# One order of a fused attention and token-mixer kernel replaced by another, its first loads kept

## The chip, the cores and the metric

The kernel runs on one core of a Trainium2 chip. The metric is the device time of one execution in microseconds, the median of several runs. The names of the engines here: PE multiplies matrices (PEld is its loading of weights), DVE and ACT work on elements, POOL is a slower engine for elements, SP issues most of the DMAs. PE writes to PSUM, of which the kernel uses eight banks; everything else lies in SBUF.

## The reference, cut to what matters

```
mod = silu(c) @ w_mod               # six rows of 512: sa, ca, ga, sb, cb, gb
h = layernorm(x) * (1 + ca) + sa    # x: 2048 tokens x 512
x = x + ga * A(h)
h = layernorm(x) * (1 + cb) + sb
x = x + gb * B(h)
# A: q, k, v = h @ wqkv, 32 heads of 16; token s attends to s, s-2, ..., s-14
#    logits = q.k / 4, masked where the index is negative; softmax over 8; times v; @ wo
# B: h = layernorm(h); u = gelu(h^T @ w1 + b1)   # over the 2048 tokens, to 1792
#    y = u @ w2 + b2, transposed back            # 1792 to 2048 tokens
```

All matrices are bf16. B mixes tokens: its first product needs every token of h before any column is complete.

## The kernel before, in words

**Tiles and stages.** The 2048 tokens are 16 tiles of 128 (st 0 to 15), in five chunks of 2, 4, 4, 4 and 2 tiles (SIZES, line 267). For each chunk `build_chunk` (lines 616 to 913) lists: the statistics of a layernorm (ln1s, ln1v, rstd1, nb1) and the normalised tile (n1); its transpose, by PE for chunks 0 and 1 (tr, hT) and by DMA for the others (xt); q, k and v (qkv, with t = 0, 1, 2) and their evacuation from PSUM (ev); the products of q with the eight shifted keys on DVE (qk, four to a chunk) and their sum over a head's 16 elements by PE (red, into the two banks psL); the maximum (max, DVE), its subtraction by PE (sub), the exponential on ACT (exp), its sum (esum), the reciprocal by logarithm and exponential (rcp, ACT), the scaling (smB, DVE), and DMAs that lay the weights out anew (a2). The values are shifted by DMA (vd). DVE multiplies weights by values (pv, four to a chunk), PE sums (pvacc), ACT copies the result to o_sb (oev), and PE multiplies by wo and adds x (wo). Then come the second layernorm (x1, ln2q, ln2m, rstd2, nb2, n2), its scaling (aff) and the third (ln3s, ln3v, rstd3, nb3, h3). The qk and pv of the four-tile chunks work on 128 x 4096 elements, those of chunks 0 and 4 on 128 x 2048.

**The token mixer** is interleaved (lines 925 to 1040): mlp1_L_F_S multiplies by w1 for block F of 14, in sweeps L over the tokens (0 to 5, 6 to 10, 11 to 15 for blocks 0 to 6; 0 to 9, 10 to 15 for the others), from tile S on; a finished sweep is parked in SBUF (park), added (padd) and put through gelu. mlp2_T multiplies by w2 for output tile T, fin adds the bias and x, st_out stores. The sweeps that start at tile 10 or 11 need h3_10 to h3_15.

**Start.** The condition c is loaded (ld_c), turned by PE (cps), and made silu(c) by an exponential on ACT (silu_exp) and three small operations on DVE (silu_dve, tile sc). modcols1 multiplies it by the 512 columns of w_mod for 1 + ca; a1col is that column, by which hT and the copies of wqkv (wsc) are scaled. modrow, mrows, st_row, ld_row and woq_s bring the other rows of mod to all partitions.

**What sets the order.** Every operation is put into a graph with the tiles that it reads and writes; `schedule` (lines 86 to 125) then emits the operations in the order of a handwritten list, ORDER (lines 191 to 249), and each engine executes its own in that order. A token is a name and a tag: `:a`, `:d`, `:p`, `:s` choose ACT, DVE, POOL or SP where an operation has alternatives. On PE `q` splits a 128-column weight load and matmul into four of 32 columns side by side (`mm`, line 522), as red, pvacc, modrow and mask always are; `n` takes the alternative without one of its matmuls. `fill:n` emits idle matmuls of n pieces of 128 columns, four pieces to one matmul (line 528); they write to a free bank and nobody reads them. Ring buffers (six PSUM banks, four `big`, five `vd`) are given out in the order of the list too, so a token's place also sets what it waits for. `locks` marks operations of DVE and is not used by `schedule`.

ld_c is added at line 429, on ACT's queue. `dma2` (line 381) adds a DMA that can go on SP's or ACT's queue.

Of the kernel before, what the change touches and what calls it, by code (L numbers as in the profile page):

```python
# [206 lines left out]
oev0_2:a qkv2_11 qkv2_02:q ev2_03:a qk2_3 qkv2_01:q red2_0 oev0_0:a wo0:q wsc2_1:a wsc2_2:a qkv2_12 ev2_11:a ev2_01:a
ev2_02:a ev2_12:a wo1 qkv2_21:q a2_1_1:a qkv2_22 x1_1:a ln2q1:a x1_0:a xt10 ln2q0:a qk2_1 qkv2_23 xt12 qk2_2 a2_1_0:s
halo_k3:a ln2m0 vd1_2 a2_1_2:s qkv3_12 a2_1_3:s pv1_2 rstd1_4 red2_1 nb1_4 vd1_0 st_row1 red2_2 red2_3 rstd2_0
ev2_22:a nb2_0 ev2_21:a qkv3_13:q ev3_13:a max2 vd1_3 pv1_0 n1_14:a vd1_1 pvacc1_2 n1_15:a qkv2_20:q ev2_20:a sub2  # L210
qkv3_22:q ev3_12:a pv1_1 qkv3_10 exp2 ev2_23:a halo_v3:a qkv3_20 n2_0:a oev1_2:a ev3_10:a esum2 rcp2 qkv3_00 ev3_22:a
# [10 lines left out]
oev3_1:a mlp1_0_2_0:q pv3_0 mlp1_0_2_2:q nb3_4 h3_4:a mlp1_0_0_0:q mlp1_0_0_2 h3_5:a mlp1_0_0_4:q qk4_0 ln2q8:a
ln2q6:a park0_0:a ln2q9:a mlp1_0_6_4:q mlp1_0_2_4:q mlp1_0_1_4:q park0_1:a pv3_2 mlp1_0_5_4:q vd3_3 pvacc3_0 oev3_0:a
mlp1_0_3_4:q ld_w2_1 park0_2:a pv3_3 red4_0 ln2m6 pvacc3_2 oev3_2:a mlp1_0_4_0:q qk4_1 pvacc3_3 ld_w1_0_1152
mlp1_0_4_2:q mlp1_0_4_4:q rstd2_6 oev3_3:a wo12:q halo_v4:p vd4_2 vd4_3 nb2_6 n2_9:a qk4_2 n2_7:d qk4_3 wo10:qn red4_1
ld_w1_0_1408 n2_6:a vd4_1 n2_8:a aff6 red4_2 red4_3 max4 park0_3:a ln3s8:d ln3s6:d x1_12:a ln3v8 wo11 vd4_0 ln3s9:d
mlp1_0_7_0 ld_w2_3 park0_4:a ln3v6 mlp1_0_7_2 park0_5:a ln3v9 x1_11:a ln2q12:a mlp1_0_8_0 mlp1_0_8_2 park0_6:a wo13:n
ln3s7:a ln3v7 sub4 mlp1_0_10_0 mlp1_0_9_0 x1_13:d exp4 rstd3_6 nb3_6 esum4 mlp1_0_8_4 ln2q13:a ln2m12 mlp1_0_10_2
mlp1_0_10_4 mlp1_0_9_2 rcp4 mlp1_0_7_4 h3_8:d rstd2_12 mlp1_0_12_0 mlp1_0_12_2 mlp1_0_12_4 smB4 a2_4_1:a a2_4_0:s
mlp1_0_9_4 a2_4_2:s h3_9:d a2_4_3:a h3_7:d nb2_12 h3_6:p mlp1_0_7_6 ln2q11:a park0_7:a x1_10:d mlp1_0_8_6 ld_w1_0_1664  # L230
ln2q10:a park0_8:a n2_13:p mlp1_0_9_6 park0_9:a n2_12:d aff12 ln2m10 rstd2_10 mlp1_0_10_6 park0_10:a ln3s13:a pv4_2
# [10 lines left out]
mlp1_2_3_11 mlp1_2_3_14 padd2_3 gelu3 ld_w1_2_640 mlp1_2_6_11 padd2_6 gelu6 padd2_2 gelu2 mlp1_2_5_11 mlp1_1_11_10
padd1_11 mlp1_2_5_14 padd2_5 gelu1 gelu11 mlp1_1_12_10 ld_w2_5 ld_w2_7 mlp1_1_13_10 gelu5 mlp2_0_0 padd1_12 gelu12
mlp2_0_0b ld_w2_2 ld_w2_9 ld_w2_13 ld_w2_11 padd1_13 gelu13 mlp2_0_0c mlp2_6_0 mlp2_4_0 gsc fin0_0 st_out0_0 fin4_0
st_out4_0 mlp2_8_0 fin8_0 mlp2_3_0 fin3_0 mlp2_2_0 fin2_0 st_out2_0 mlp2_1_0 fin1_0 mlp2_7_0 st_out3_0 fin6_0
st_out6_0 fin7_0 mlp2_10_0 fin10_0 st_out7_0 mlp2_11_0 mlp2_5_0 st_out1_0 fin5_0 st_out5_0 mlp2_14_0 fin11_0
# [829 lines left out]
```

## Time and profile before

| | |
|---|---|
| median of 3 runs | 201.75 us |
| lowest, highest | 201.44, 202.0 us |
| the profiled execution | 202.11 us |
| its span in the profile | 200.4 us |
| DMA, mean | 179 GB/s, 35.95 MB |

The span goes from the first instruction to the last; the 1.7 us around it are not in the profile. All lines of the profile name line 142 for the kernel's own instructions, because one helper issues them all, so a row is recognised by its tiles: psS are the six PSUM banks, psL the two of the logits, big the products of DVE, h the normalised tiles, xx the tokens, hT the transposed tiles, wst the ring of weights. A row of the timeline has its start, its length, the engine, the operation, output and inputs with their shapes, and how many such rows it merges; in square brackets stands the idle time ahead of it and who ended it. Rows of PE overlap, so that the step from start to start is what a matmul costs.

### The profile page before, as it was taken

How to read it: one execution, taken by the hardware profiler on the slowest of the kernel's cores; microseconds unless marked ns; L12 is line 12 of the kernel's file. 1: busy time of each engine (PE TensorE's matmuls, PEld its weight loads, DVE VectorE, ACT ScalarE, POOL GpSimd, SP SyncE). 2: the span in 40 equal slices, each digit the busy share in tenths (PEclk: the TensorE clock that was granted, in tenths of full speed). 3: DMA queues.
4: the chain of work that ended last, by engine and by line, in shares of the span. 5: the costliest groups of instructions: out<-in, count | busy, mean ns of one | idle time of the engine just before them, and what ended most of it. 6: DMA issues, size and time to landing. Idle time of an engine off the chain costs nothing.

```text
span 200.4 us, 4572 instructions
## 1 busy us (share of the span) xinstructions
PE 191.0 (95%) x1818; PEld 95.8 (48%) x1836; DVE 159.6 (80%) x241; ACT 128.6 (64%) x306; POOL 18.6 (9%) x45
## 2 busy tenths in 40 slices
PE   3999999999899999999999999999999999999993
PEld 1387754554344455534444444444444444444453
DVE  2689999999999999999999999986655253726554
ACT  4879897998899999999999698953670000000000
POOL 4155001200100001030000200320000000000000
PEclk9999999999999999999999999999999999999999
DMA  5999594826758745549399268568999201011611
GB/s 161 341 355 350 176 240 127 160 56 185 300 143 321 220 167 194 176 112 311 64 310 257 36 184 196 160 186 234 338 244 298 85 26 52 27 52 52 174 52 52
DMA packets 53889, 35.95 MB, mean 179 GB/s; under 512 B 24428, under 2 KB 50668, under 8 KB 53868
## 3 DMA queue, kind: packets, MB, share of 16 engines
q1 hardware_dynamic: 52228, 35.21, 61.2%
q10 hardware_dynamic: 1640, 0.46, 1.0%
q8 instruction: 14, 0.23, 0.5%
q14 instruction: 7, 0.06, 0.1%
HBM read 22.55 MB, written 2.10 MB: 123 GB/s over the span
## 4 chain that ended last, share of the span: by engine, by line
PE 69%; DVE 22%; issue 4%; DMA 1%; ACT 1%; ACTq 0%; DVEq 0%
PE psS L142 67%; DVE big L142 14%; PE psL L142 3%; DVE st L142 2%; DVE h L142 2%; DMA c_t<-in_c_dram 1%; DVE mv L142 1%; ACT h L142 1%; DVE lsb L142 1%; DVE m L142 1%; DVE nb L142 0%; ACTq L142 0%; DVE woq L142 0%; DVE hT L142 0%; ACT rb L142 0%
## 5 line engine op out<-in xcount | busy, mean ns | idle before, releaser
L142 PEld LDWEIGHTS <-wst 128*128 128x128 bf16 (+1 forms) x536 | 34.9, 101 | 33.7 <-issue 4.0
L142 PE MATMUL psS<-h,wst 128*128 128x512 bf16 (+1 forms) x333 | 50.3, 380 | 0.5 <-issue 0.3
L142 DVE TENSOR_TENSOR big<-q_sb,k_f 128x4096 bf16<-128x4096 bf16 (+1 forms) x20 | 36.6, 1859 | 0.4 <-ACT q_sb L142 0.4
L142 DVE TENSOR_TENSOR big<-a2sb,vD 128x4096 bf16<-128x4096 bf16 (+1 forms) x20 | 36.5, 1860 | 0.2
L142 PE MATMUL psS<-hT,w_qkv 128*32 128x512 bf16 (+3 forms) x360 | 29.7, 346 | 0.0
L142 DVE SCALAR_TENSOR_TENSOR h<-psS,bcol,rows_bc 128x512 f32<-128x512 f32 (+2 forms) x17 | 12.1, 710 | 22.1 <-PE psS L142 20.6
L142 PEld LDWEIGHTS <-w_qkv 128*32 128x32 bf16 (+1 forms) x402 | 19.4, 109 | 17.8 <-issue 4.4
L142 PE MATMUL psS<-gT,big 128*128 128x512 bf16 x110 | 24.7, 379 | 0.1
L142 PEld LDWEIGHTS <-big 128*128 128x128 bf16 x144 | 12.0, 97 | 13.5
L142 ACT ACTIVATE junk<-xx 128x512 bf16<-128x512 bf16 x26 | 16.3, 627 | 3.3 <-DVE xx L142 1.4
L142 PE MATMUL psS<-woq,o_sb 128*32 128x512 bf16 (+1 forms) x107 | 15.7, 380 | 0.9 <-ACT o_sb L142 0.6
L142 ACT ACTIVATE gT<-psS,bcol 128x512 bf16<-128x512 f32 x14 | 9.0, 685 | 8.1 <-DVE psS L142 8.0
L142 POOL TENSOR_SCALAR h<-xx,rs,nb 128x512 bf16<-128x512 bf16 x9 | 6.9, 766 | 75.6 <-DVE nb L142 36.5
L142 DVE TENSOR_TENSOR psS<-psS,gT 128x512 f32<-128x512 f32 x14 | 9.3, 695 | 5.0 <-PE psS L142 5.0
L142 ACT ACTIVATE h<-xx,nb,rs 128x512 bf16<-128x512 bf16 x16 | 12.4, 808 | 0.5 <-DVE nb L142 0.4
L142 PEld LDWEIGHTS <-ident 128*32 128x32 bf16 (+1 forms) x137 | 7.0, 102 | 10.5 <-issue 5.9
L142 PE MATMUL psS<-ident 128*128 128x512 bf16 (+1 forms) x35 | 10.6, 450 | 1.4 <-POOL epscol L142 1.4
L142 PE MATMUL psS<-hT,wst 128*32 128x512 bf16 (+2 forms) x110 | 11.7, 352 | 0.1
L142 DVE TENSOR_TENSOR h<-h,xx 128x512 bf16<-128x512 f32 (+2 forms) x17 | 11.1, 653 | 0.6
L142 DVE TENSOR_TENSOR h<-h,rows_bc 128x1024 bf16<-128x1024 bf16 (+2 forms) x16 | 10.9, 689 | 0.4
L142 DVE BATCH_NORM_STATS2 st<-xx 128x6 f32<-128x512 bf16 x12 | 7.9, 680 | 3.9 <-DMA xx<-in_A_x_dram 3.8
L142 ACT ACTIVATE v_sb<-psS,qvb 128x512 bf16<-128x512 f32 (+1 forms) x20 | 11.0, 595 | 0.0
(100 smaller groups left out, 242.9 us busy)
## 6 DMA issues: line engine op xcount, KB each, us to landing
vD<-v_sb SPq DMA_DIRECT2D x12, 524.5 KB, 4.0
big<-in_B_w_dram SPq DMA_DIRECT2D x4, 896.0 KB, 7.4
vD<-v_sb SPq DMA_DIRECT2D x8, 268.5 KB, 3.8
wst<-in_B_w_dram SPq DMA_DIRECT2D x3, 640.0 KB, 5.0
out_dram<-h SPq DMA_DIRECT2D x15, 128.0 KB, 1.8
wst<-in_B_w_dram SPq DMA_DIRECT2D x2, 800.0 KB, 4.8
xx<-in_A_x_dram SPq DMA_DIRECT2D x6, 256.0 KB, 7.9
gT<-in_w_mod_dram SPq DMA_DIRECT2D x4, 384.0 KB, 5.9
```

The costliest lines, as they stand in the source:

```text
L142: r = fn(*a, **k)
```

## The change

ORDER is replaced as a whole, and ld_c goes through `dma2` with the tag `:a`. The operations are the same ones. The first thirteen loads, ld_x_1_2 to ld_x_3_12, keep their queue and order; then the list has ld_wqkv2, ld_x_4_14 and ld_wrow3, where it had ld_b2, ld_wo1 and ld_wqkv2. The idle matmuls ahead of the first products are 56 and 12 pieces, where they were 4, 64 and 4, and 13; behind them 2 pieces, where they were 1, 1, 18 and 14; and 25 pieces come behind the last matmul. silu_exp stands behind rstd1_0 on ACT, where it was the first activation. Of the engine tags some thirty differ, among them: to DVE ln1s1, ln1s8, hT1_2, qvb_cp0, mrows0 and n2_11; away from DVE ln1s0, n1_5, hT1_1, hT1_3 and wsc2_0 (to ACT), n1_4 and n2_14 (to POOL); from ACT to POOL n1_1, n1_8, n1_12, halo_v1, halo_v3, wsc1_0 and h3_15; from POOL to ACT n1_6, n1_9, wsc0_2, halo_v2 and h3_14. The tag `q` is on other matmuls than before. The lists, cut to the lines that are spoken of:

```diff
 ORDER = """
-ident ld_x_1_2:a halo0 ld_c consts ld_x1:s ld_x0:s ld_x_1_4:s act_table ln1s3:d fill:4 cps ld_wmod1 silu_exp silu_dve
-fill:64 ln1s1:a ln1s2:a ln1s0:d ln1v1 ld_x_2_8 ln1v0 ln1s4:d ld_wqkv0 rstd1_0 nb1_0 n1_1:a fill:4 ln1v4 n1_0:p ln1s5:d
-ln1v2 ln1v5 ln1v3 rstd1_1 nb1_1 ld_x_2_6 modcols1 n1_2:d n1_5:d ln1s8:a a1col wsc0_3:p n1_4:d tr0_0 hT0_1:a hT0_3:a
-n1_3:d hT0_0:a fill:13 hT0_2:a ld_wqkv1 ld_wmod0 ln1s9:d ld_x_3_10 ln1s6:d tr1_0 tr1_2 hT1_2:a ln1v6 qkv0_02 ln1v9
-hT1_0:a qkv0_12 qkv0_10 ln1s7:d ln1v7 ln1v8 rstd1_2 hT1_3:d wsc1_0:a ev0_12:a modcols0 sab:a ld_x_3_12 nb1_2 n1_8:a
-qkv0_00 qvb0 wsc0_0:p ev0_10:a ld_b2 ld_wo1 hT1_1:d qkv1_00 ln1s11:d ln1s10:d ln1s13:d qkv1_10:q ln1v11 ln1v10
-qvb_cp0:a ev0_00:a ln1s12:a ev0_02:d qkv1_13 ld_wqkv2 qkv0_20 ln1v13 qk0_3 qk0_2 ev1_13:a qk0_0 qvb1 ln1v12 qkv0_22:q
-ld_wrow0 red0_0 ev1_00:a qkv1_03:q ev1_10:a qk0_1 red0_1 red0_2 red0_3 mask qvb_cp1:a ev0_20:a ev0_22:a wsc1_2:p
-halo_v1:a qk1_0 ev1_03:a wsc1_3:a qkv1_11:q ld_wmod2 wsc2_3:a modrow0 ld_b1 mrows0:a ev1_11:a ld_wrow2 qkv1_02 max0
...
-red1_1 a2_0_1:a n1_9:p wsc2_0:d ln1s15:a ln1v14 nb1_3 n1_11:a qkv1_23:q mrows1 qkv1_21 ev1_21:a red1_2 red1_3 xt8
-ev1_23:a fill:1 n1_10:p qkv1_20 ev1_20:a ev1_22:a qkv2_13 qkv2_10 wsc0_1:p vd0_2 ev2_13:a ln1v15 vd0_1 max1 sub1
...
-biascols_cp:a pvacc0_1 pv0_3 pvacc0_2 pvacc0_3 ev2_10:a ev2_00:a qk2_0 n1_13:a n1_12:a ld_row0 woq_s rcp1 smB1
...
-smB2 aff0 qk3_0 vd2_1 fill:1 vd2_0 oev1_0:a oev1_1:a pvacc1_3 ev3_11:a qk3_1 qkv3_23:q oev1_3:a a2_2_2:s ln3s1:a
...
-qkv3_21:q ev3_21:a wo5 red3_1 pv2_3 x1_5:a vd2_2 qk3_3 qkv4_20:q red3_2 qkv4_22 red3_3 qkv4_12 fill:18 ln2q5:a
-ld_w1_0_512 ln2q2:a ln2m2 pv2_0 pvacc2_0 vd3_0 ev4_20:a ln3s0:a ln3v0 ev4_12:a rstd2_2 ev4_22:a ln3v1 qkv4_02 oev2_0:a
...
-ld_w1_0_0 n2_5:a rcp3 smB3 pvacc2_2 fill:14 a2_3_0:s a2_3_1:s a2_3_3:s n2_4:a qkv4_00:q oev2_2:a rstd3_0 aff2 pvacc2_1
...
-pvacc4_0 pvacc4_1 n2_11:a mlp1_0_13_0:q pvacc4_2 pvacc4_3 n2_10:a mlp1_0_13_2:q park0_11:a mlp1_0_13_4 oev4_0:a
...
-ln2s15 rstd2_14 nb2_14 ln2v15 n2_14:d rstd3_10 aff14 rstd2_15 nb2_15 inj1_4:qn ln3v13 park0_12:a mlp1_1_3_6 park0_13:a
...
-h3_15:a ld_w1_2_0 park1_1:+ mlp1_1_2_10 park1_2:+ mlp1_1_7_10 park1_3:+ park1_4:+ park1_5:+ mlp1_1_8_10 mlp1_1_10_10
...
-st_out10_0 st_out11_0 ld_w2_15 fpre mlp2_9_0 mlp2_13_0 fin14_0 st_out14_0 st_out8_0 mlp2_12_0 fin9_0 st_out9_0 fin13_0
-st_out13_0 mlp2_15_0 fin12_0 st_out12_0 fin15_0 st_out15_0 mlp2_15_1 fin15_1 st_out15_1 mlp2_15_2 fin15_2 st_out15_2
+ld_x_1_2:a ld_c:a ld_x1:s consts ident cps halo0 ld_x0:s ld_x_1_4:s act_table ln1s1:d ln1v1 fill:56 ln1s3:d ln1v3
+ld_wmod1 ln1s0:a ln1v0 ln1s4:d ln1s5:d ld_x_2_8 ln1v4 ld_wqkv0 ln1s2:a ln1v5 rstd1_0 ln1v2 nb1_0 n1_0:p ld_x_2_6
+silu_exp silu_dve ln1s9:d modcols1 rstd1_1 nb1_1 n1_5:a n1_1:p ln1s8:d a1col tr0_0 ld_wqkv1 hT0_0:a n1_3:d n1_4:p
+hT0_1:a n1_2:d ln1s7:d fill:12 ln1v9 ln1v8 tr1_2 ld_wmod0 ld_x_3_10 ld_x_3_12 hT0_3:a hT0_2:a tr1_0 qkv0_02 hT1_3:a
+ld_wqkv2 hT1_0:a wsc0_1:p ln1v7 ln1s6:d wsc0_3:p wsc1_0:p ln1v6 ld_x_4_14 ld_wrow3 rstd1_2 qkv0_10 hT1_1:a nb1_2 ld_b2
+wsc1_3:a hT1_2:d qkv0_12 ev0_12:a ln1s11:d modcols0 sab:a qkv0_00 ld_wrow2 wsc1_2:p ld_wo2 wsc0_0:p wsc1_1:p ld_wrow0
+ld_wo3 ln1s10:d ln1v11 qvb0 ld_wo1 ln1s13:d ln1s12:a ln1v10 qvb_cp0:d qkv1_00 ev0_00:a ln1v13 qkv1_13 qkv1_10 ev0_02:d
+qvb1 ln1v12 rstd1_3 ev0_10:a qk0_2 qkv0_20 ev1_00:a qk0_3 qkv1_03:q qk0_0 red0_0 qkv0_22:q qvb_cp1:a wsc2_3:a ld_wmod2
+n1_6:a ev1_10:a qk0_1 red0_1 ev1_03:a red0_2 qk1_0 ev1_13:a ev0_20:a ev0_22:a red0_3 mask ld_wrow1 n1_9:a qkv1_02 max0
...
+n1_8:p vd0_0 vd0_3 halo_v1:p wsc0_2:a mrows0:d ln1v15 ln1v14 rstd1_4 nb1_3 n1_12:p mrows1 xt8 qkv2_00 n1_11:a qkv2_10
+a2_0_0:s ev1_23:a ev2_00:a nb1_4 a2_0_3:s ev2_10:a max1 sub1:q exp1 a2_0_1:s n1_13:a pv0_3 vd0_2 pv0_2 ev1_21:a
+qkv2_11:q ev1_22:a qk2_0 ev2_11:a wsc2_2:a qkv1_20:q ev1_20:a pv0_0 fill:2 qkv2_02:q pvacc0_2 esum1 rcp1 n1_14:a vd0_1
+qkv2_13 qkv2_01 red2_0 pv0_1 ev2_01:a pvacc0_3 oev0_2:a st_row0 n1_10:p ev2_13:a pvacc0_0 pvacc0_1 oev0_0:a ld_wo0
+ld_row0 xt10 xt12 vd1_1 smB1 a2_1_2:s qkv2_12:q ev2_12:a ev2_02:a qkv2_03 ev2_03:a woq_s wo0:q a2_1_3:a qk2_1 red2_1
...
+red2_2 rstd2_0 red2_3 qkv3_13:q a2_1_1:s halo_k3:a ev3_02:a wsc2_0:a pv1_1 ev3_13:a qkv3_00 vd1_3 nb2_0 n2_1:p qkv3_10
...
+ld_row1 qkv2_21 pvacc1_3 oev1_3:a smB2 pvacc1_0 aff0 oev1_0:a qkv3_03:q qk3_0 ev2_21:a wo4 wo2 xt14 ln3s0:a a2_2_1:s
...
+a2_2_3:s a2_2_0:s red3_1 ln2m2 ev3_22:a rstd2_2 qkv4_00:q qkv3_21:q vd2_2 red3_2 vd2_3 ev4_00:a ev3_21:a red3_3 pv2_0
...
+mlp1_0_13_0:q pv4_3 park0_12:a oev4_0:a pvacc4_3 n2_11:d ln3v13 oev4_2:a aff10 ln3s11:d inj1_3:n mlp1_0_13_2:q
...
+nb2_14 n2_14:p ln3v10 rstd3_10 inj1_6:qn mlp1_0_13_6 ld_w1_1_896 ln2s15 ln2v15 rstd2_15 mlp1_1_0_6 nb3_10 aff14 ln3v12
...
+inj1_1:n rstd3_15 nb3_15 mlp1_1_3_10 nb3_14 h3_14:a mlp1_1_2_10 mlp1_1_1_6 mlp1_1_1_10 inj1_4:qn h3_15:p mlp1_1_4_6
...
+fin11_0 st_out11_0 mlp2_9_0 fin9_0 mlp2_2_0 fin2_0 st_out2_0 fin6_0 st_out4_0 mlp2_8_0 fin8_0 st_out8_0 st_out9_0
+mlp2_10_0 mlp2_12_0 fin12_0 st_out6_0 fin10_0 mlp2_13_0 fin13_0 st_out10_0 mlp2_14_0 fin14_0 st_out13_0 mlp2_15_0
+fin15_0 mlp2_15_1 fin15_1 st_out12_0 mlp2_15_2 fill:20 fill:5 st_out14_0 st_out15_0 st_out15_1 fin15_2 st_out15_2
 """
...
 
     wmodA = big_r[0][:, 0:KT * 2 * D].rearrange("p (k n) -> p k n", k=KT)
     s_wm = _Slot("big")
-    add("act", 0.55, lambda: nc.scalar.dma_start(c_t[:], c[0].rearrange("(t p) -> t p", p=P)), writes=["c_t"],
-        name="ld_c", lat=2.0)
+    dma2(c_t[:], c[0].rearrange("(t p) -> t p", p=P), D * 4, ["c_t"], "ld_c")
     for st in range(SIZES[0]):
         dma2(xx[:, st, :], x_view[:, st, :], P * D * 2, [("xx", st)], f"ld_x{st}")
     first = None
```

More of the change, by code (lines that the diff above doesn't have):

```diff
@@ L207 @@
[L207 to L211, printed above, removed]
@@ L222 @@
[L222 to L226, printed above, removed]
@@ L227 @@
[L227 to L231, printed above, removed]
@@ L242 @@
[L242 to L246, printed above, removed]
@@ new lines @@
+mlp1_0_8_4 mlp1_0_7_2 n2_13:d aff12 mlp1_0_7_4 mlp1_0_7_6 park0_7:a mlp1_0_8_6 park0_8:a ln2m10 rstd2_10 pv4_2
+mlp1_0_9_6 park0_9:a pv4_1 mlp1_0_10_6 ld_w1_0_1664 mlp1_0_11_0 mlp1_0_11_2 ln3s13:a park0_10:a mlp1_0_11_4
+mlp1_0_11_6:q ld_w1_1_0 mlp1_0_12_6:q park0_11:a nb2_10 pvacc4_2 n2_10:a pv4_0 pvacc4_0 inj1_0:n pvacc4_1 ld_w1_1_640
+mlp1_0_13_0:q pv4_3 park0_12:a oev4_0:a pvacc4_3 n2_11:d ln3v13 oev4_2:a aff10 ln3s11:d inj1_3:n mlp1_0_13_2:q
+ln3s12:a mlp1_0_13_4:q wo14 x1_14 ln3v11 ln2s14 ld_w2_2 wo15 ln2v14 ln3s10:a x1_15 rstd2_14 inj1_2:qn mlp1_1_2_6
@@ new lines @@
+nb2_14 n2_14:p ln3v10 rstd3_10 inj1_6:qn mlp1_0_13_6 ld_w1_1_896 ln2s15 ln2v15 rstd2_15 mlp1_1_0_6 nb3_10 aff14 ln3v12
+nb2_15 n2_15:p ln3s14:d ln3v14 h3_10:a h3_11:a rstd3_12 aff15 inj1_5:qn nb3_12 h3_12:p h3_13:p ln3s15:d ln3v15
+mlp1_1_3_6 mlp1_1_6_6 mlp1_1_0_10 mlp1_1_5_6 mlp1_1_5_10 park0_13:a ld_w2_1 park1_0:+ mlp1_1_6_10 ld_w1_2_0 rstd3_14
+inj1_1:n rstd3_15 nb3_15 mlp1_1_3_10 nb3_14 h3_14:a mlp1_1_2_10 mlp1_1_1_6 mlp1_1_1_10 inj1_4:qn h3_15:p mlp1_1_4_6
+mlp1_1_4_10 park1_1:+ park1_2:+ ld_w2_5 mlp1_1_10_10 ld_w1_1_1408 park1_3:+ park1_4:+ padd1_10 mlp1_1_8_10 mlp1_1_7_10
```

43 lines of the change are left out of this document (27 added, 16 removed).

## The prediction

> **What bounds the kernel now.** I read the page first, then the windows, then the chain of work that ended last, and the timeline of the places where the change can act.
>
> ```profile
> span 200.4 us, 4572 instructions
> PE 191.0 (95%) x1818; PEld 95.8 (48%) x1836; DVE 159.6 (80%) x241; ACT 128.6 (64%) x306; POOL 18.6 (9%) x45
> PE   3999999999899999999999999999999999999993
> DVE  2689999999999999999999999986655253726554
> ```
>
> PE is busy for 95% of the span, but that is a mean over stages. In the slices (forty equal parts, tenths busy) DVE stands at nine from the fourth to the twenty-seventh; only afterwards is PE alone at nine. The windows, cut where the chain changes, give that in numbers (the columns are PE, weight loads, DVE, ACT and POOL, each busy us and count).
>
> ```profile
> 17.80:122.00 104.20, 101.67 (x1322) 51.11 (x1333) 102.45 (x123) 96.38 (x235) 7.42 (x11) 1.00 0.68 194
> 122.00:132.10 10.10, 10.10 (x48) 4.57 (x47) 9.24 (x28) 8.99 (x26) 3.03 (x4) 1.00 0.53 119
> 132.10:197.60 65.50, 64.91 (x324) 30.95 (x328) 36.79 (x56) 10.15 (x15) 0.00 (x0) 1.00 0.49 141
> ```
>
> From 17.8 to 122 us, the attention stage, DVE is busy for 102.45 of 104.20 us, so only 1.75 us of it is idle; PE is idle for 2.53 us. From 132.1 us PE has all its inputs and nothing but its own rows: that part keeps its length in any order. So the time is the start (to 17.8) plus DVE's work in the attention stage plus a PE part of fixed length, and the change must shorten one of the first two. The chain of waits says the same, with DVE's products (2.25 us each) on it in the middle and an unbroken row of PE from 121.76 on:
>
> ```profile
> 46.96 4.49 DVE big L142 x2
> ...
> 121.76 12.03 PE psS L142 x55
> ```
>
> **The change part by part.** *Start.* Ahead of the first real matmuls stand idle ones.
>
> ```profile
> 4.10 6.58 PE L142 MATMUL psS<-ident 128*128 128x512 bf16 x17
> 4.50 0.15 PEld L142 LDWEIGHTS <-ident 128*128 128x128 bf16 x1 [0.28 <-issue]
> 4.92 0.15 PEld L142 LDWEIGHTS <-ident 128*128 128x128 bf16 x1 [0.28 <-issue]
> 9.62 0.57 PEld L142 LDWEIGHTS <-ident 128*128 128x128 bf16 x3 [0.28 <-issue]
> 10.52 0.54 PE L142 MATMUL psS<-sc,big 128*128 128x1 bf16 x16
> 7.46 0.20 ACT L142 ACTIVATE rs<-lv 128x2 f32<-128x2 f32 x1
> 7.97 0.77 POOL L142 TENSOR_SCALAR h<-xx,rs,nb 128x512 bf16<-128x512 bf16 x1 [4.73 <-DVE nb L142]
> 11.18 1.11 DVE L142 TENSOR_SCALAR h<-xx,rs,nb 128x512 bf16<-128x512 bf16 x2
> 17.84 2.36 PE L142 MATMUL psS<-hT,wst 128*128 128x512 bf16 x21
> 18.80 2.36 DVE L142 TENSOR_TENSOR big<-q_sb,k_f 128x2048 bf16<-128x2048 bf16 x2
> ```
>
> Seventeen idle matmuls (64 and 4 pieces, four to a matmul) run from 4.10 to 10.52. The weight load of each has its own row; from 4.50 to 9.62 there are twelve steps, 0.427 each, and the three loads from 9.62 lie (0.57 - 0.15) / 2 = 0.21 apart: PE runs at half rate until about 9.6. The new order keeps 14. Thirteen slow ones and a fast one end at 4.10 + 13 x 0.427 + 0.21 = 9.87, so modcols1 (the row of 16 at 10.52) comes **0.65 us earlier**. Two things could hold it. The condition's exponential is issued behind rstd1_0, at 7.46 + 0.20; with 0.17 on ACT and half a us on DVE, sc is there at about 8.4, which 1.4 us of idle matmuls hide; with that cover gone modcols1 could not start ahead of 8.4. n1_1 goes from ACT to POOL behind n1_0: two of 0.77 from 7.97 end at 9.5, hidden too. fill:12 instead of fill:13 is one piece less beside a wait. Behind modcols1, a1col, the two norms of 1.11, the transposes and four qkv groups move along; but ld_x_2_6 and ld_x_3_12 land no earlier, and ACT takes one hT more ahead of qvb0. I take **-0.45** at qkv1_00 and at the first qk (18.80); the bounds are 0 and -0.65. The loads cost nothing: up to ld_x_3_12, the thirteenth, queue and order are the same; the fourteenth is ld_wqkv2 instead of ld_b2, so "fourteen" holds only in part. ld_c already was on ACT's queue.
>
> [...]
>
> *PE's idle matmuls and switches later.* fill:18 and fill:14 go, and 2 pieces come.
>
> ```profile
> 75.17 0.62 PE L142 MATMUL psL<-big,group 128*32 128x512 bf16 x8
> 75.71 1.06 PE L142 MATMUL psS<-hT,w_qkv 128*128 128x256 bf16 x8
> 76.61 1.14 PE L142 MATMUL psS<-ident 128*128 128x512 bf16 x6
> 77.68 0.62 PE L142 MATMUL psS<-big,group 128*32 128x512 bf16 x8
> 82.34 0.93 PE L142 MATMUL psS<-ident 128*128 128x512 bf16 x5
> 83.21 1.07 PE L142 MATMUL psS<-hT,w_qkv 128*32 128x256 bf16 x32
> 85.64 0.59 PE L142 MATMUL psS<-woq,o_sb 128*128 128x512 bf16 x2 [0.61 <-ACT o_sb L142]
> ```
>
> They last 77.68 - 76.61 = 1.07 and 83.21 - 82.34 = 0.87 us. A change between matmuls in four 32-column tiles (a tag q, red, pvacc) and whole ones costs too: red3_3 starts at 75.17 with two steps of 0.21 and its successor comes at 75.71, so the switch is 0.1 us; the orders have 46 and 44 of them. PE thus loses 1.9 + 0.2 us of work before the projection wo. I cost that at **0**: at 85.64 wo waits for o_sb, which comes from DVE's last pv through ACT, so PE would only wait longer. The full 2.1 counts where DVE is no longer late.
>
> *DVE's and ACT's share.* Some thirty operations change engine. The rows of one each:
>
> ```profile
> L142 DVE TENSOR_SCALAR h<-xx,rs,nb 128x512 bf16<-128x512 bf16 x7 | 3.2, 480 | 0.0
> L142 DVE TENSOR_SCALAR w_qkv<-h,a1col 128x512 bf16<-128x512 bf16 x1 | 0.3, 346 | 0.0
> L142 DVE TENSOR_SCALAR mrows<-psS 128x128 bf16<-128x128 f32 x1 | 0.3, 291 | 0.0
> L142 ACT ACTIVATE h<-xx,nb,rs 128x512 bf16<-128x512 bf16 x16 | 12.4, 808 | 0.5 <-DVE nb L142 0.4
> L142 ACT ACTIVATE junk<-xx 128x512 bf16<-128x512 bf16 x26 | 16.3, 627 | 3.3 <-DVE xx L142 1.4 <-issue 1.4
> L142 DVE TENSOR_TENSOR big<-q_sb,k_f 128x4096 bf16<-128x4096 bf16 (+1 forms) x20 | 36.6, 1859 | 0.4 <-ACT q_sb L142 0.4
> ```
>
> Behind the first qk DVE loses wsc2_0 (0.35) and n2_14 (0.4), and gains mrows0 (0.29) and n2_11 (0.4); ln1v12 moves ahead of qk: **-0.1 us**. The twenty qk and twenty pv are all still there. ACT loses a norm (0.81) and one pair of statistics (2 x 0.63 and two reads, 1.5): 2.3 us of its 96; the rest of its exchanges cancel within 0.1. ACT is not the bound, but DVE waits for it, 0.4 us at q_sb in the last row. Of DVE's 1.75 idle us I take this named wait, **-0.4**, for what a lighter ACT and PE give; the bounds are 0 and the 1.75. Two moves that could make DVE wait have room: rcp1 must come before smB1, and four pv of 1.2 and a qk of 2.25 lie between max1 and smB1, 7 us; qkv2_21, the last of chunk 2's v, now comes just ahead of smB2, but pv2_0 stands behind aff0 and four qk, ten us later. Past SP's and POOL's queues I found no load that newly stands behind a wait and is needed within it: ld_row0 is behind st_row0 as before, and ten us of DVE's work lie between mrows0 and woq_s.
>
> *The end of attention and the tail.*
>
> ```profile
> 112.89 0.77 POOL L142 TENSOR_SCALAR h<-xx,rs,nb 128x512 bf16<-128x512 bf16 x1 [2.01 <-DVE nb L142]
> 113.25 0.56 DVE L142 TENSOR_SCALAR h<-xx,rs,nb 128x512 bf16<-128x512 bf16 x1
> 112.24 0.41 DVE L142 TENSOR_SCALAR h<-h,rs,nb 128x512 bf16<-128x512 bf16 x1
> 131.14 0.81 ACT L142 ACTIVATE h<-h,nb,rs 128x512 bf16<-128x512 bf16 x1 [0.36 <-DVE nb L142]
> ```
>
> h3_15, the last input of the token mixer, is ready at 131.95, and PE starts the first sweep that reads it at 132.1 (the third window's cut), as its sixth matmul: 1 us of slack. h3_15 now goes to POOL behind h3_12 and h3_13, and h3_14 from there to ACT: three on POOL and one on ACT as before, so 0, and the slack covers a few tenths. The order of mlp2, the stores and the seven idle matmuls behind the last piece (6 x 0.21 + 0.06 = 1.3 us from about 197.5, in a span that ends at 200.4 with the last store) cost 0, the store being their cover.
>
> **Sum:** -0.45 - 0.1 - 0.4 = **-0.95 us**. The profiled execution took 202.11 us for a span of 200.4; it would become 201.16. It stands 0.36 above the median of 201.75, so the prediction is **200.8 us**.
>
> **The rivals.** *Nothing arrives* (201.6): the start's gain is eaten and DVE's sum is the same. The clock may open behind the shorter run: then 14 x 0.427 ends at 10.08 and the transposes follow at half rate; or DVE waits for tiles 12 and 13. For it: DVE's terms are only 0.1 by rows. Against: modcols1 waited for nothing but idle matmuls. *DVE's idle time goes as well* (199.4): all of 1.75 and the start's 0.45, and 0.1: -2.3. For it: PE and ACT both become lighter by 2 us. Against: much of the idle time is steps of 0.05 between dependent short operations. *POOL takes DVE's port* (slower): in the rows above DVE's norm took 0.56 beside POOL's and 0.41 alone, and at 11.18 two took 1.11. By the tags POOL gets 24 such operations instead of 21 and one more halo copy, n1_12, n1_10 and two halos among them in the stage where DVE is full. If each blocks DVE for its length, 3 x 0.77 and about 0.4 for the copy, an estimate of half a norm, are 2.7 us, and the time is 203.5; from two blocks on, 1.5, the sum turns positive. Against: most of them fall beside operations of DVE that read PSUM (max, mrows1), where the rows show no delay.
>
> [...]
>
> **How the numbers follow.** The forecast has 0.38, nothing arrives 0.15, DVE's idle time 0.13, POOL 0.34. A measurement of this kernel can tell about 0.3% from no change, 0.6 us: faster is below 201.15, slower above 202.35. Faster: 0.33 of the forecast's 0.38 and 0.13, **0.46**. Slower: 0.32 of POOL's case, **0.32**. Same: the rest, **0.22**. The range 199.6 to 203.0 leaves out the larger half of the idle-time case and the upper third of POOL's.
>
> **What would show it.** Right: modcols1 at about 9.9, qkv1_00 at 17.4, the first qk at 18.4; DVE over 98% busy until wo14; PE idle by some 2 us more in the stage; wo14 at about 121 instead of 122; the part behind it as long as before. Wrong: a DVE row of qk or pv longer than its 2.25 or with POOL named ahead of it; the first sweep on h3_15 waiting on POOL; a stage longer than 104.2 between qkv1_00 and wo14, which would mean a new wait on DVE, or PE now the bound.

## The result, and the profile after

The kernel after takes **203.29 us** (median of 10 runs, 201.78 to 204.71) beside 201.63 for the kernel before (10 runs, 201.25 to 202.12). The ratio is 1.0085, 95% interval 1.0056 to 1.0113: **slower by 0.85%**, where 200.8 us and a range of 199.6 to 203.0 were forecast. The runs spread over 2.9 us, those of before over 0.9. The profiled execution took 203.89 us for a span of 201.9.

The page of the kernel after, its span, PE's slices, the slices of PE's granted clock, the chain's shares by engine, and the group of qk:

```profile
span 201.9 us, 4707 instructions
...
PE   1989999999999995999999999999999999999994
...
PEclk9999999999999998899999999999999999999999
...
PE 62%; DVE 20%; DMA 6%; ACT 5%; issue 3%; SPq 2%; DVEq 0%; ACTq 0%
...
L142 DVE TENSOR_TENSOR big<-q_sb,k_f 128x4096 bf16<-128x4096 bf16 (+1 forms) x20 | 36.4, 1858 | 0.1
```

Three things are to be seen. PE's sixteenth slice (75.7 to 80.8 us) has a hole, and this slice and the next have a lower clock; before, both rows stood at nine there. DMA has 6% of the chain, where the page of before gives it 1%; half of the 6% are the transfers of weights a2sb, the other half the first loads of x. And the qk rows take 1858 ns, 1 ns less than before, although POOL has twelve norms at 772 ns instead of nine: POOL's further work did not make DVE's products longer. The other way round there is a delay. POOL's copies of 128 x 64 elements, one along a qk row of DVE (62.52 to 64.80 us) and one at the end of such a row:

```profile
62.76 2.15 POOL L142 COPY v_sb<-v_sb 128x64 bf16<-128x64 bf16 x1 [8.95 <-ACT v_sb L142]
24.66 0.24 POOL L142 COPY v_sb<-v_sb 128x64 bf16<-128x64 bf16 x1 [7.95 <-ACT v_sb L142]
```

The first of the windows with the same cuts as before:

```profile
17.80:122.00 104.20, 101.23 (x1380) 50.83 (x1382) 101.01 (x122) 95.36 (x229) 8.70 (x11) 0.98 0.67 186
```

DVE's busy time in it fell from 102.45 to 101.01, so its idle time rose from 1.75 to 3.19. The waits of DVE in this window name 1.9 of it:

```profile
DVE big L142 <- DMA a2sb<-lsb: 0.9, 1, 0.9
DVE mv L142 <- ACT junk L142: 0.6, 1, 0.6
DVE big L142 <- issue: 0.4, 1, 0.4
```

The 0.4 at q_sb that the prediction wanted to remove is gone, and 1.9 has come. The start, in the timeline of the kernel after, looks better than forecast in this profile:

```profile
4.21 4.76 PE L142 MATMUL psS<-ident 128*128 128x512 bf16 x14
...
8.81 0.54 PE L142 MATMUL psS<-sc,big 128*128 128x1 bf16 x16
...
17.93 1.23 DVE L142 TENSOR_TENSOR big<-q_sb,k_f 128x2048 bf16<-128x2048 bf16 x1
```

All of the span can be cut at three points of DVE's rows: the start of the first qk, the start of the last pv, and the end of its last row. Summed over DVE's rows between these points (us, profiled executions; the last four columns belong to experiments that are told below):

| | before | after | fetch_gone | w1_behind | w1_fetch_gap | before_fetch2 |
|---|---|---|---|---|---|---|
| to the first qk | 18.80 | 17.93 | 18.38 | 17.76 | 17.77 | 18.01 |
| DVE's work, first qk to last pv | 99.04 | 98.89 | 98.66 | 98.65 | 98.69 | 99.07 |
| DVE's idle time in it | 1.46 | 3.19 | 2.76 | 1.76 | 1.72 | 1.43 |
| last pv to the end of DVE's last row | 78.35 | 78.15 | 78.15 | 78.15 | 78.15 | 78.57 |
| from there to the span's end | 2.74 | 3.74 | 2.71 | 3.94 | 2.72 | 3.83 |
| span | 200.4 | 201.9 | 200.7 | 200.3 | 199.1 | 200.9 |

From before to after: -0.87 - 0.15 + 1.73 - 0.20 + 1.00 = +1.51 us. In this pair of profiles the gains are there; **two losses outweigh them: DVE's idle time and the last microsecond**.

**The first loss, DVE's idle time.** SP's queue in the timelines, before and after, from the end of chunk 2's softmax on:

```profile
58.53 2.18 SPq L142 DMA_DIRECT2D vD<-v_sb  x3
62.72 3.27 SPq L142 DMA_DIRECT2D a2sb<-lsb  x4
66.03 0.61 SPq L142 DMA_DIRECT2D vD<-v_sb  x1
66.69 0.59 SPq L142 DMA_DIRECT2D wst<-in_B_w_dram  x1
```

```profile
48.98 1.67 SPq L142 DMA_DIRECT2D rows_bc<-scratch  x1
60.45 1.28 SPq L142 DMA_TRANSPOSE hT<-h  x1
61.83 0.67 SPq L142 DMA_DIRECT2D a2sb<-lsb  x1
62.55 0.59 SPq L142 DMA_DIRECT2D wst<-in_B_w_dram  x1
63.24 0.56 SPq L142 DMA_DIRECT2D vD<-v_sb  x1
63.85 0.65 SPq L142 DMA_DIRECT2D a2sb<-lsb  x1
64.56 1.22 SPq L142 DMA_DIRECT2D vD<-v_sb  x1
65.83 2.41 SPq L142 DMA_DIRECT2D a2sb<-lsb  x2
68.28 2.06 SPq L142 DMA_DIRECT2D vD<-v_sb  x2
```

Before, the four transfers of weights (a2sb) go out together, behind three transfers of values (vD) that SP issued from 58.53 us on, and the load of the mixer's weights (wst) goes behind them. After, SP stands from 50.65 to 60.40 us at xt14 (the transpose), and then a load of wst and two of values are mixed in among the four. SP's longest wait between 48 and 75 us is for PE, whose last products on chunk 2 (qkv2_21) run from 59.32 to 60.3:

```profile
SPq L142 <- PE psS L142: 9.7, 1, 9.7
```

The time from issue to landing of the a2sb (least, median, most; the profile has it for three of the four before and for two of the four after), before and after:

```profile
DMA to landing us min/median/max: 2.1/2.3/3.4
```

```profile
DMA to landing us min/median/max: 6.9/7.1/7.3
```

What DVE waits for then starts late, and so does what hangs on it. PE's row behind the hole, and the 3.41 us ahead of and behind 79.11 us, with PE's granted clock in the third column from the right:

```profile
78.85 0.83 PE L142 MATMUL psS<-big,group 128*32 128x512 bf16 x8 [1.68 <-DVE big L142]
```

```profile
75.70:79.11 3.41, 1.33 (x30) 0.51 (x18) 3.41 (x4) 3.41 (x7) 0.82 (x2) 1.00 0.68 182
79.11:82.52 3.41, 3.41 (x28) 2.02 (x24) 3.41 (x2) 2.10 (x6) 0.00 (x0) 0.50 1.01 357
```

PE idles for 2.08 of 3.41 us and has half the clock in the next 3.41; the wait for ACT's junk, 0.6 us, follows at 88.2.

**The second loss, the end.** The stores of the last four or five pieces, by issue time (least, median, most, in ns) and landing, before and after; then the one row of the DMA queues that only the kernel after has from 196 to 202 us:

```profile
L142 SPq DMA_DIRECT2D out_dram<-h x4: 332/332/382, 195.8 to 197.8; - x4
DMA to landing us min/median/max: 1.5/1.6/1.7
```

```profile
L142 SPq DMA_DIRECT2D out_dram<-h x5: 332/383/1356, 193.6 to 199.3; - x5
DMA to landing us min/median/max: 1.8/2.4/2.9
```

```profile
q8 instruction: 1, 0.02, 1.7%
```

That is a packet of 16,384 bytes, read here as PE's own instructions being fetched; the experiments, which change only the number of PE's rows, make it come and go. It starts at 197.24, 0.35 us after the start of mlp2_15_2, and ends at 198.84. In its time the issue of st_out15_1 takes 1.36 us, so that the last store is issued at 199.31, where the kernel before issues it at 197.78. PE has 3786 rows after (1893 weight loads and as many matmuls) and 3672 before, twice the 1836 weight loads of its page, which lacks some records of matmuls. The difference is more matmuls in four pieces, and the seven idle ones at the end. Such packets come every 250 rows on average (15 of them for 3786 rows after, 14 for 3672 before); before, the last one came at 181.84 us.

### The profile page after: what moved, and what is told of

Same layout as the page of the kernel before. It is cut to its first block, busy times and chain, and to the rows that moved or that the text cites. A ratio compares the mean times of both kernels' runs of the same rounds, so it can differ in the third digit from the quotient of the medians.

```text
span 201.9 us, 4707 instructions
## 1 busy us (share of the span) xinstructions
PE 191.3 (95%) x1893; PEld 95.9 (48%) x1893; DVE 159.3 (79%) x240; ACT 127.1 (63%) x300; POOL 22.8 (11%) x49
## 4 chain that ended last, share of the span: by engine, by line
PE 62%; DVE 20%; DMA 6%; ACT 5%; issue 3%; SPq 2%; DVEq 0%; ACTq 0%
PE psS L142 58%; DVE big L142 11%; DVE h L142 4%; DMA a2sb<-lsb 3%; PE psL L142 3%; DMA xx<-in_A_x_dram 3%; SPq L142 2%; DVE st L142 2%; ACT v_sb L142 1%; ACT o_sb L142 1%; ACT junk L142 1%; DVE mv L142 1%; DVE m L142 1%; ACT lsb L142 1%; ACT k_f L142 0%
## 5 line engine op out<-in xcount | busy, mean ns | idle before, releaser
L142 PE MATMUL psS<-h,wst 128*32 128x512 bf16 (+1 forms) x368 | 51.1, 380 | 0.3 <-ACT xx L142 0.2
L142 DVE TENSOR_TENSOR big<-a2sb,vD 128x4096 bf16<-128x4096 bf16 (+1 forms) x20 | 36.4, 1857 | 1.5 <-DMA a2sb<-lsb 0.9
L142 DVE TENSOR_TENSOR big<-q_sb,k_f 128x4096 bf16<-128x4096 bf16 (+1 forms) x20 | 36.4, 1858 | 0.1
L142 PE MATMUL psS<-hT,w_qkv 128*32 128x512 bf16 (+3 forms) x384 | 30.9, 350 | 0.0
L142 PEld LDWEIGHTS <-w_qkv 128*32 128x32 bf16 (+1 forms) x426 | 19.9, 109 | 16.4 <-issue 3.6
L142 ACT ACTIVATE junk<-xx 128x512 bf16<-128x512 bf16 x24 | 15.1, 627 | 3.4 <-DVE xx L142 1.3
L142 PE MATMUL psS<-woq,o_sb 128*32 128x512 bf16 (+1 forms) x124 | 16.6, 380 | 0.4 <-ACT o_sb L142 0.4
L142 POOL TENSOR_SCALAR h<-xx,rs,nb 128x512 bf16<-128x512 bf16 x12 | 9.2, 772 | 57.7 <-DVE nb L142 38.5
L142 PEld LDWEIGHTS <-group 128*32 128x32 bf16 x288 | 7.0, 96 | 10.2 <-issue 3.6
L142 DVE BATCH_NORM_STATS2 st<-xx 128x6 f32<-128x512 bf16 x13 | 8.7, 680 | 3.8 <-DMA xx<-in_A_x_dram 3.7
L142 PE MATMUL psS<-big,group 128*32 128x512 bf16 (+1 forms) x160 | 9.7, 346 | 1.8 <-DVE big L142 1.7
## 6 DMA issues: line engine op xcount, KB each, us to landing
vD<-v_sb SPq DMA_DIRECT2D x12, 524.5 KB, 6.3
```

Of the source, the lines that this page charges most:

```text
L142: r = fn(*a, **k)
```

## The experiments

The theory was that these two losses are the whole of it, each with its own cause: bytes queued ahead of a2sb, and an instruction packet among the last stores. The rivals were that POOL's work makes DVE's longer, the idle matmuls at the end, and the new start. Each kernel is the one after with the edit shown, if nothing else is said; ratios are to the kernel before on the same chip, with 95% intervals.

**a2_first.** Two of the four small transfers of weights change places, so that the one that was held to be needed first goes first.

```diff
-... xt14 ln3s0:a a2_2_1:s qk3_1 ... a2_2_3:s a2_2_0:s red3_1
+... xt14 ln3s0:a a2_2_0:s qk3_1 ... a2_2_3:s a2_2_1:s red3_1
```

> The kernel after, with a2_2_0 and a2_2_1 exchanged in the list, so that the DMAs of the weights of chunk 2 are issued in the order in which DVE's products pv2_0, pv2_2, pv2_3, pv2_1 read them. Theory (a late transfer): in the trace of the kernel after, a2_2_0 is issued at 66.51 us, last of its four, lands 6.3 us later, DVE waits 0.9 us for it, and PE idles 1.84 us behind sub3. Issued first, it lands by about 68, so DVE's row of 0.9 behind a2sb is gone, max3 and the rest of chunk 3 come 0.9 us earlier, and the span is 0.9 to 1.5 us shorter: about 202.1 us by the median of 203.29. Rival (POOL's tiles take the port of DVE, or the DVE rows are just longer): the transfer is not what sets the end, and the time stays at 203.3; DVE's wait turns into another wait, on a2_2_1 or on PE.

Measured 203.47 us, ratio 1.0107 (1.0082 to 1.0133). The waits of DVE still have

```profile
DVE big L142 <- DMA a2sb<-lsb: 0.7, 1, 0.7
```

and the landing is still at 7.2 us. This form of the theory falls: it is not the order of the small transfers among themselves. The kernel says why: every pv product reads all four of its chunk's weights (line 827 of the kernel after), so DVE's first product waits for the last of the four, whichever that is.

**w1_behind.** The large load goes behind chunk 2's weights and values.

```diff
-... x1_3:a ld_w1_0_0 biascols ...
-... red3_2 vd2_3 ... red3_3 ...
+... x1_3:a biascols ...
+... red3_2 vd2_3 ld_w1_0_0 ... red3_3 ...
```

> The kernel after, with ld_w1_0_0 moved from ahead of vd2_0 to behind vd2_3, so that the load of 768 KB stands behind the weights and the values of chunk 2 on SP's queue. In four traces of that queue order DVE's first product of chunk 2 waited 0.2, 0.7, 0.9 and 1.2 us for a2sb, and a2_2_2, a2_2_3 landed 6 to 8 us after their issue, where the old order had 2.1 to 3.4; exchanging two of the small transfers among themselves did not help (0.74 us). Theory (bytes queued ahead): 768 KB at some 350 GB/s are 2.2 us, so a2sb lands before DVE asks for it, DVE's row on a2sb is gone, and the stage of the attention is 0.7 us shorter: about 202.6 us beside 203.3. Rival (the transfers wait for something else, the DMA transpose xt14 ahead of them or the values vd2): landings stay at 6 to 8 us, the wait stays, 203.3 us.

Measured 202.26 us, 1.0038 (1.0020 to 1.0056), about 0.9 us less than the kernel after by the two ratios. The a2sb (two of the four) land in

```profile
DMA to landing us min/median/max: 4.1/4.5/4.8
```

with the transpose and two loads of vD still ahead of them, and of DVE's waits only the one of 0.4 on "issue" is left. PE's clock in the window from 80 to 85 us is 1.00, where eight matmuls of 128 x 256 take 1.04 us (1.91 at half the clock in the kernel after), and the wait for junk is gone too. The wait for a2sb is thus the misplaced load's. For the clock and the wait for ACT one profile says little, since those of a2_first and fetch_gone, with the load where it was, have neither. Over all runs it holds: the mean clock is 0.991 or 0.992 in 10 of the 40 runs of the kernels with the load ahead of the weights and PE's hole left open (after, a2_first, fetch_gone, no_tail_fill), which are 0.7 to 1.7 us longer than the others of their kernel by the medians, and it is so in none of the 48 runs with the load moved.

**w1_in_hole.** To see whether it is the bytes and not this place in the list, the same load goes ahead of xt14 instead, in the kernel w1_fetch_gap of below.

```diff
-ld_row1 qkv2_21 ... red3_2 vd2_3 ld_w1_0_0 ... red3_3
+ld_row1 ld_w1_0_0 qkv2_21 ... red3_2 vd2_3 ... red3_3
```

> w1_fetch_gap with ld_w1_0_0 moved again, from behind vd2_3 to ahead of xt14, where SP stands still from 50.65 to 60.40 us and the DMA engines moved 2 GB/s from 55 to 60 us. Theory (bytes queued ahead of a2sb, not the list as such): the load's 768 KB go through in the hole, the four a2 of chunk 2 land as in w1_fetch_gap, 4 to 5.5 us behind their issue, DVE shows no row on a2sb, and the time is the same 201.1 us. Rival (the ring of weights has no free buffer that early, so that the load blocks SP and xt14 behind it): DVE waits in chunk 2 again, 0.5 us or more.

Measured 201.35 us, 0.9999 (0.9980 to 1.0017), beside 0.9980 (0.9962 to 0.9998) for w1_fetch_gap: the same within the intervals. The a2sb land in

```profile
DMA to landing us min/median/max: 4.6/4.7/4.8
```

and DVE has no wait on them. It is the bytes ahead in the queue, not the place in the list.

**fetch_gone.** The 25 idle pieces at the end stay; 48 rows of PE go elsewhere.

```diff
-mlp1_0_11_6:q ld_w1_1_0 mlp1_0_12_6:q park0_11:a
+mlp1_0_11_6 ld_w1_1_0 mlp1_0_12_6 park0_11:a
```

> The kernel after, with mlp1_0_11_6 and mlp1_0_12_6 as whole matmuls instead of four pieces of 32 columns each: 24 matmuls and 24 weight loads fewer on PE, the same product, the same columns. Theory (instruction fetch): in the trace of the kernel after, one instruction packet of 16 KB starts at 197.24 us, 30 PE rows ahead of the end of PE's program; the store issued at 197.87 then takes 1.36 us to issue where its neighbours take 0.33 to 0.38, and the span ends 4.2 us after the last useful matmul instead of 3.2. With 48 rows fewer, fewer than the 256 rows that lie between two such packets are left, the packet is not there, and the tail is 1.0 us shorter: about 202.3 us. Rival (the 25 idle pieces behind the last matmul hold something up): the packet is not the cause, the tail stays 4.2 us, the time 203.3.

Measured 202.03 us, 1.0038 (1.0017 to 1.0060). The last instruction packet of PE lies at 177.06 us, none comes behind it, and the last stores are as before:

```profile
L142 SPq DMA_DIRECT2D out_dram<-h x4: 332/332/382, 196.1 to 198.1; - x4
```

The end is 2.71 us long again, with all idle matmuls in place, so these are not the cause. That 256 rows lie between two packets was the author's figure, and no run shows it: in the profile of the kernel after it is 124 to 376, 251 on average. The first loss stays: DVE waits 1.2 us ahead of the first pv of chunk 2. The profile names vD for it, not a2sb; the product reads both, and both stand behind the load.

**no_tail_fill.** The other way round: only the idle matmuls go.

```diff
-fin15_0 mlp2_15_1 fin15_1 st_out12_0 mlp2_15_2 fill:20 fill:5 st_out14_0
+fin15_0 mlp2_15_1 fin15_1 st_out12_0 mlp2_15_2 st_out14_0
```

> The kernel after without fill:20 and fill:5 behind the last matmul. Theory (instruction fetch): the packet starts 16 rows ahead of the last useful matmul, so it is there without the fills too, and the tail stays about 4.2 us: no change, 203.3 us. Rival (the idle matmuls are what holds up the last stores): the tail goes back to 3.2 us, 202.3 us.

Measured 202.37 us, 1.0054 (1.0029 to 1.0079). Here the theory's number was wrong: the packet is gone, and the end is 2.72 us long. Fourteen rows fewer were enough. By itself this run agrees with the rival as well; only fetch_gone tells the two apart.

**before_fetch and before_fetch2.** The kernel before gets the packet. The first has 120 rows more in four sweeps; the second 84 rows in three of them, and 30 rows of idle matmuls at the end.

```diff
-mlp1_1_11_10 ... mlp1_2_5_14 ... mlp1_1_12_10 ... mlp1_1_13_10
+mlp1_1_11_10:q ... mlp1_2_5_14:q ... mlp1_1_12_10:q ... mlp1_1_13_10:q
```

```diff
-mlp1_2_5_14 ... mlp1_1_12_10 ... mlp1_1_13_10 ... mlp2_15_2 fin15_2
+mlp1_2_5_14:q ... mlp1_1_12_10:q ... mlp1_1_13_10:q ... mlp2_15_2 fill:3 fill:3 fill:3 fill:3 fill:3 fin15_2
```

> The kernel before, with mlp1_1_11_10, mlp1_2_5_14, mlp1_1_12_10 and mlp1_1_13_10 as four pieces of 32 columns each: 60 matmuls and 60 weight loads more, the same products and columns, at 0.1 to 0.2 us for two changes of the tiling. Nothing else differs. Theory (instruction fetch): a 16 KB packet comes about every 250 PE rows, the last one in the trace of before at 181.84 us; 120 rows more move one more packet into the last 2 us of PE's program, the last stores issue late and land late, and the kernel is 1.0 to 1.2 us slower: 202.6 us. Rival (the packets are harmless): 0.2 us at most.

> The kernel before, with mlp1_2_5_14, mlp1_1_12_10 and mlp1_1_13_10 in pieces of 32 columns (84 PE rows more) and 15 idle matmuls of 128 columns behind the last matmul (30 rows more). In before_fetch the 16 KB packet came at 195.37 us, 0.5 us ahead of the start of mlp2_15_2, and cost 0.2 us at the tail; in the kernel after it comes 0.35 us behind that start and costs 1.0. Theory (the packet costs what it delays): with fewer rows ahead of it the packet falls about 0.4 us behind the start of mlp2_15_2, the issue of st_out15_1 takes over 1.2 us, and the tail behind DVE's last row is 3.6 to 3.9 us instead of 2.74: about 202.5 us. Rival (the loss of 1.0 us belongs to the new order of the stores or to the idle matmuls, which fetch_gone kept without a loss): the tail stays at 2.7 to 3.0, 201.8 us.

before_fetch measured 201.98 us, 1.0027 (1.0011 to 1.0042), half a microsecond instead of one: the packet came at 195.37, half a microsecond ahead of mlp2_15_2, and the end was 2.96 us long. The two changes of tiling cost 0.2. before_fetch2 measured 202.69 us, 1.0066 (1.0043 to 1.0090), and there the packet came at 197.37:

```profile
L142 SPq DMA_DIRECT2D out_dram<-h x4: 332/332/1501, 195.2 to 197.2; - x4
DMA to landing us min/median/max: 1.7/2.4/3.2
```

This time it is the last store whose issue takes 1.5 us, and the end is 3.83 us long. The length of the end is as expected, the place is not: the packet came 1.6 us behind the start of mlp2_15_2 instead of 0.4. The packet costs what it delays (0.2 us where it came ahead of mlp2_15_2, 1.1 where it came with the last store), in the old order of the stores as in the new one.

**w1_and_fetch and w1_fetch_gap.** Both repairs at once; and both with PE kept busy in its hole.

```diff
-n2_5:a pv2_2 sub3 exp3 pv2_3
+n2_5:a pv2_2 sub3 fill:28 exp3 pv2_3
```

> w1_behind and fetch_gone in one: ld_w1_0_0 behind vd2_3, and mlp1_0_11_6, mlp1_0_12_6 as whole matmuls, so that PE's program has 48 rows fewer. Theory: both terms add up, 0.7 from DVE's wait and 1.0 from the last stores, about 201.3 us, within 0.3% of the kernel before or a little under it, since the earlier start (0.4 to 0.9) stays. Rival (the loss sits in longer DVE rows or in POOL's port): only what fetch_gone alone gave, 202.0 us.

> w1_and_fetch with 28 idle pieces (7 matmuls, 1.5 us by 0.216 us each) behind sub3, where PE idles 1.84 us for pv2_2. Theory (clock): in the trace of the kernel after PE's granted clock was 0.75 in the 5 us behind this gap, the matmuls there took 1.3 us longer, and DVE waited 0.6 us for ACT at 88.2; runs with a mean clock of 0.992 are some 0.5 us longer than those with 1.0. With PE kept busy all runs show 1.0, and the spread of the times is smaller: 201.1 us. Rival: the gap never sets the end, since DVE is the chain there, 201.3 us and the same spread.

Measured 201.44 us, 0.9986 (0.9970 to 1.0003), and 201.06 us, 0.9980 (0.9962 to 0.9998). The two terms add up: 1.0085 less 0.0047 twice is 0.9991. The spread, 2.9 us in the kernel after, is 1.1 in both. The gap's idle matmuls give nothing that can be told from zero, since the two intervals overlap. w1_fetch_gap is the fastest kernel here, by 0.2% with an interval that just leaves out 1; as the best of eleven that is no clear gain.

**gap_fill.** The idle matmuls in the hole alone.

> The kernel after with 28 idle pieces behind sub3 alone, all else as in the kernel after. Theory (the clock is a small part): no run shows a mean clock of 0.992 any more, which in four of ten runs of the kernel after cost some 0.5 us, so the median falls by 0.2 to 0.4, to about 203.0 us; DVE's wait for a2sb (0.2 to 1.2 us) and the late last stores stay. Rival (the clock is the main part, and the late a2sb only shows its effect): 202.3 us or less.

Measured 202.29 us, 1.0038 (1.0012 to 1.0064), the number of the rival. But its 14 rows more also moved the packet from 197.24 to 196.11, and the end is 2.97 us long instead of 3.74: by the profiles that is 0.8 of the 0.9 us between the two ratios. The run changed two things and can't size the clock. It does show that none of its twelve runs had a mean clock under 1.00, where three of the ten of the kernel after (not four) had 0.992.

**start_after.** The new list up to the first qk, then the old one.

```diff
+ld_x_1_2:a ld_c:a ... qvb1 ln1v12 rstd1_3 ev0_10:a
+n1_8:a qkv0_20 qk0_3 qk0_2 ev1_13:a qk0_0 qkv0_22:q red0_0 ...
```

> The first part of the new list, up to the first qk, followed by everything that is left of the old list in the old order. Theory: the new start is worth the 0.9 us by which the first qk comes earlier in the trace of the kernel after (17.93 for 18.80), and what the kernel after loses lies behind it: 201.63 less 0.9 is 200.7 us. Rival (the new start moves loads, and the loss of the kernel after comes from them): no gain, 201.6 us or more, with waits on vD, a2sb or weights in the stage of the attention.

Measured 203.62 us, 1.0107 (1.0083 to 1.0131): a loss of 1.7 to 2.6 us instead of a gain. The first qk came at 18.88, and DVE's waits are other ones:

```profile
DVE big L142 <- DMA a2sb<-lsb: 1.4, 1, 1.4
DVE big L142 <- ACT q_sb L142: 1.0, 1, 1.0
```

These are the rival's number and its sign. But the waits are not those of the kernel after (this one on a2sb is in chunk 4, at 118 us), and w1_and_fetch and w1_in_hole have the same start with both losses mended and lose nothing that can be told from zero, so the start is not what the kernel after loses by. The old middle does not fit the new start; what the start is worth by itself this run does not say.

## Why the prediction was wrong

*What bounds the kernel.* Right: DVE to the last pv, then a row of PE. But the end of the program is not PE's row: it is that row and the stores behind it, and this last part was no step of the sum. (PE's row itself, forecast to keep its length, came out 0.20 shorter by the table.) Of the prediction's signs, wo14 came at 122.48 us instead of about 121, though the first qk came earlier than forecast: the stage got longer by a new wait on DVE, as the last of its signs of being wrong has it.

*Start, -0.45.* The mechanism was right (modcols1 waits only for idle matmuls), the size is uncertain. The three rows of the 14 idle matmuls, of modcols1 and of the first qk say -0.87 in one profile, but the same instructions gave other times in other runs, w1_behind first and fetch_gone second:

```profile
4.09 4.49 PE L142 MATMUL psS<-ident 128*128 128x512 bf16 x14
8.42 0.54 PE L142 MATMUL psS<-sc,big 128*128 128x1 bf16 x16
```

```profile
4.09 6.13 PE L142 MATMUL psS<-ident 128*128 128x512 bf16 x14
10.04 0.56 PE L142 MATMUL psS<-sc,big 128*128 128x1 bf16 x16
```

The same fourteen thus take 4.5 to 6.1 us; what decides it no run shows. With the old start, modcols1 came at 10.52 in the profile of before and at 9.08 in that of before_fetch. Over ten profiles of the new start, start_after's 18.88 among them, the first qk lies at 17.76 to 18.95, mean 18.30; over three of the old one at 18.01 to 18.80, mean 18.30 too. So the profiles show no gain by the start, the few tenths of the forecast are within their spread, and *nothing arrives* was nearly right on this term.

*DVE's swaps, -0.1.* Right in kind: -0.15 to -0.4 in the table's second line. *PE's later idle matmuls, 0.* Right in that removing them did no good; that PE's granted clock could stand at 0.50 behind a hole at 76 us was not seen.

***DVE's idle time, -0.4: the first step that failed.*** The named wait on q_sb did go. But the sentence "Past SP's and POOL's queues I found no load that newly stands behind a wait and is needed within it" is false. ld_w1_0_0 stood there in the list, ahead of three of the four a2 of chunk 2, behind xt14, which waits for the last products on chunk 2. ld_w1_0_0 is needed late itself, but what stands behind it is not. The cover was counted in time and rightly (ten us between smB2 and pv2_0; the rows give 10.8). What was not counted is what the transfers have to carry in it. In the DMA issues of the kernel after between 60 and 73 us stand

```profile
vD<-v_sb SPq DMA_DIRECT2D x4, 524.5 KB, 7.8
wst<-in_B_w_dram SPq DMA_DIRECT2D x1, 768.0 KB
a2sb<-lsb SPq DMA_DIRECT2D x4, 64.0 KB, 7.1
```

and ahead of the last a2sb lie 768 KB, two of 524.5 and three of 64, together 2.0 MB. The rate in forty slices of the same 13 us is

```profile
GB/s 0 0 0 0 0 158 216 208 197 43 141 59 85 47 69 142 262 306 312 318 299 345 393 396 432 388 360 457 373 373 372 290 380 417 425 421 413 417 422 349
```

Nothing moves until 61.6 us, little until 65, and from there 2.0 MB at 300 to 430 GB/s take 5 to 7 us, to 70 or 72. The two landings that the profile has lie at 71.2 and 72.7, and DVE asks at 72.1. The term came out as +1.73 in the profile; by w1_behind the misplaced load is worth 0.9 us of the median, with what the clock adds in some runs. Nor did the -0.4 come with the load out of the way: DVE idles 1.72 to 1.76 us in the four kernels with the load moved, where the three profiles of the old list have 1.43 to 1.46. A new 0.4 on "issue" stands in the place of the one on q_sb, and the other 0.3 are short gaps that no wait names.

***The end, 0: the second step that failed.*** "The order of mlp2, the stores and the seven idle matmuls behind the last piece [...] cost 0, the store being their cover." PE had time for them, but the store was no cover for all they did; the rows that they and the split matmuls added moved an instruction packet onto the stores: +1.0 in the profile, 0.9 of the median by fetch_gone.

*The rivals.* *POOL takes DVE's port* gave 203.5, near the measured time, by luck: the qk and pv rows did not grow (1858 and 1857 ns, 1859 and 1860 before), and DVE has no waits on POOL. That POOL blocks DVE for the length of each operation, from which the 2.7 us were added up, was the author's estimate, and no run shows it, nor a port that the two share: DVE's work from the first qk to the last pv is 98.89 us, 99.04 before. What the rows of these products show is a delay of POOL: of its rows behind the first qk only a copy lies along a qk row, and it took 2.15 us, where the two others took 0.24. *DVE's idle time goes as well* went the other way. The three kernels without the two losses have ratios of 0.9980 to 0.9999, that is 0 to 0.4 us of the 0.95 that were forecast: without them, too, the forecast would have been too large.

*Left open.* DVE idles 0.4 us ahead of the first pv of chunk 4 in all kernels of the new list (but start_after), put down to "issue"; no run was made on it. The clock's own part of the first loss isn't sized. DVE's wait for the weights of chunk 2 varies from 0.2 to 1.2 us: by the semaphore counts of the traces, fifteen of the sixteen parts of the last a2sb are in by 71.88 us in the kernel after, 71.95 in fetch_gone and 71.95 in no_tail_fill, the sixteenth at 72.85, 73.57 and 72.41; what holds it back is not known. And why an instruction packet holds up an issue on SP is argued from the coincidence in six traces (four with the packet late and an issue of 1.24 to 1.58 us, two with it earlier and 0.69 to 0.70), not shown from inside.

## What to carry to other kernels

When a list is reordered, go through each DMA queue and add up the bytes that stand ahead of every transfer somebody waits for, from the moment at which the queue starts to move again: time between issue and need is no cover if it is shorter than the bytes ahead take (here 5 to 7 us for 2.0 MB). Count the rows that a change adds to the program of the engine that issues most instructions (here PE), and look where the last instruction packet falls; here a place among the last stores cost 1.0 to 1.2 us, and 14 to 120 rows more or less moved it. And take the start of a kernel from several profiles (here the first qk lay at 17.76 to 18.95 us) before a few tenths of it are used in a sum.
